# Attention and a token/channel mixer in one kernel: subtraction on VectorE, tiles in three pools, early reciprocals by way of DRAM

## The chip, the cores and the metric

The kernel runs on one core of one Trainium2 chip. The metric is the device time of one execution in microseconds, lower is better. A core has TensorE (PE, matmuls; its weight loads are listed as PEld), VectorE (DVE), ScalarE (ACT), GpSimd (POOL) and SyncE (SP), which here issues nearly all DMA transfers. Each runs its own list of instructions in order and waits on semaphores for the others. TensorE writes into PSUM, eight banks; all else lives in SBUF, 128 rows.

## The reference, cut to what matters

```
def phi(x):                                   # x: 8 batches, 8 heads, 576 tokens, 64
    proj = einsum('bhsd,df->bhsf', x, w_phi)  # 128 features
    proj = proj - max(abs(proj), axis=-1, keepdims=True)
    return concatenate([exp(proj), exp(-proj)], axis=-1)
q_p, k_p = phi(q), phi(k)
kv  = einsum('bhsf,bhsd->bhfd', k_p, v)
z   = sum(k_p, axis=2)
num = einsum('bhsf,bhfd->bhsd', q_p, kv)
den = einsum('bhsf,bhf->bhs', q_p, z)[..., None] + 1e-06
x   = num / den                               # heads side by side: 576 x 512
h   = relu(x.T @ w_tok1) @ w_tok2             # 576 -> 256 -> 576
u   = x + h.T
out = u + relu(u @ w_ch1) @ w_ch2             # 512 -> 1536 -> 512
```

All is float32, and the mixer's weights arrive as 64-bit floats.

## The kernel before, in words

Heads go in pairs: 32 pairs of two heads, four pairs to a batch. Five generators emit the program, and `weave` runs them side by side by shares written out by hand (each `yield` names a cost): `keys`, `queries`, `token_stream`, `load_weights`, `channel_stream`. The Tile framework then orders the instructions of each engine by its own simulated clock, so the final order on an engine is a planner's; an edit in one stage can shift the order in others.

*Attention.* For a group of two 128-token units, `less_max` multiplies by `w_phi` into PSUM, takes the largest absolute value of each row on VectorE (L226) and subtracts it. For the first four pairs (`i < PLAIN`) the product is one plain float32 matmul and stays in PSUM; `base` says which half of the rows holds the data, D for keys and 0 for queries. For the other pairs (`base is None`) both operands are split into a high and a low part of float32r, three fast matmuls replace one slow one (`mm3`), and the subtraction is a GpSimd instruction (L237) on a copy in SBUF.

For the plain pairs the subtraction goes another way. GpSimd negates the maximum (L229, two columns). For keys, ScalarE takes exp(proj - max) and exp(-proj + max) straight from PSUM with the negated or plain maximum as bias, one instruction for each unit and sign (L285). For queries, ScalarE writes proj - max with an Identity and a bias, one instruction for each unit (L235); TensorE transposes that and ScalarE takes the exponentials from PSUM (L371).

`add_kv` sums k_p and v over tokens into PSUM (L308) and copies the result to SBUF. `turn` and `numerators` give, for each half of a pair's tokens (k = 0: 320 tokens, k = 1: 256), the numerators and the denominators. For the first eight pairs (`i < EARLY`) ScalarE writes den with 1e-6 added (L406), later VectorE does (L408). Every denominator stands in 64 rows, one for each column of its head. When both heads are there (j == 1), VectorE takes the reciprocal of the whole 128 x 320 or 128 x 256 tile (L410) and GpSimd multiplies x by it (L411). den has one buffer.

*Weights.* `convert` loads a block of 64-bit floats into one of a few staging buffers (SP, L125), ScalarE takes the absolute value (L131), four VectorE instructions build the float32 (L132 to L135), ScalarE and GpSimd split it into high and low (`split`, L72 and L75). 33 such blocks are turned in the first part of the run, while the first pairs go through attention.

*Mixer.* `token_mix` needs all four pairs of a batch, `channel_mix` takes chunks of 256 tokens. Both are made of `mm3` (L81). They hold most of TensorE's work.

*Tiles.* Tiles that TensorE reads as its moving operand are made by `streamed`: 16 floats of padding on both sides. `column` rounds the small maxima up to 32 floats. Except for the constant pool all tiles lie in one pool, `wk`.

Of the kernel before, what the change touches and what calls it, by code (L numbers as in the profile page):

```python
# [8 lines left out]
F32 = mybir.dt.float32  # L9
F32R = mybir.dt.float32r  # L10
U32 = mybir.dt.uint32
# [6 lines left out]
P = 128  # L18
B, H, S, D = 8, 8, 576, 64
NP = H // 2  # L20
F = 128
# [21 lines left out]
def mixer_kernel(ctx, tc, qk, vm, vt, w_phi, w1, w2, wc1, wc2d, out):  # L43
    nc = tc.nc

    cst = ctx.enter_context(tc.tile_pool(name="cst", bufs=1))
    wk = ctx.enter_context(tc.tile_pool(name="wk", bufs=2))
    ps_w = ctx.enter_context(tc.tile_pool(name="ps_w", bufs=1, space=PSUM))
    ps_k = ctx.enter_context(tc.tile_pool(name="ps_k", bufs=1, space=PSUM))
# [3 lines left out]
    REST = dict(tag="rest", bufs=3)  # L53

    def streamed(pool, shape, dtype, **kw):

        n = 1
        for k in shape[1:]:
            n *= k
        t = pool.tile([P, n + 32], dtype, **kw)[:, 16:16 + n]  # L60
        if len(shape) == 3:
            t = t.rearrange("p (a b) -> p a b", a=shape[1])
        return t

    def column(pool, n, **kw):

        return pool.tile([P, 32], F32, **kw)[:, :n]

# [17 lines left out]
    make_identity(nc, ident)  # L86
    eps = cst.tile([P, 40], F32, name="eps")[:, :1]
    nc.gpsimd.memset(eps, 1e-6)
    wp2 = streamed(cst, [P, 2, F], F32R, name="wp2")
    wp = cst.tile([P, F], F32, name="wp")  # L90
# [5 lines left out]
    w1_l = cst.tile([P, 5, T], F32R, name="w1_l")  # L96
    w2_h = streamed(cst, [P, NT, S], F32R, name="w2_h")
    w2_l = streamed(cst, [P, NT, S], F32R, name="w2_l")
    wc1_h = cst.tile([P, NC_, E], F32R, name="wc1_h")
# [4 lines left out]
    for j in range(2):  # L104
        t = cst.tile([P, 672], F32, name=f"v{j}")[:, :650].rearrange("p (u j d) -> p u j d", u=5, j=2)
        nc.gpsimd.memset(t[:, 4], 0.0)
        nc.gpsimd.memset(t[:, 0:4, :, D:], 1.0)
        for i in range(2):
            nc.gpsimd.memset(t[i * D:(i + 1) * D, 4, i, D:], 1.0)
        vtiles.append(t)  # L110
# [3 lines left out]
    def convert(hi, lo, srcs, name, tag=None):  # L114
# [13 lines left out]
        top, low = raw[:, :, 1], raw[:, :, 0]  # L128
        m = streamed(wk, [P, 512], U32, tag="bits", name=f"bits{name}", bufs=3)[:w, :n]

# [60 lines left out]
    def less_max(ts, units, name, base=None):  # L191
# [25 lines left out]
        if base is None:  # L217
            part = wk.tile([P, 2, F], F32, tag="part", name=f"part{name}")
            nc.scalar.copy(part[:, :n], ps[:, :n, 1])
            pr = wk.tile([P, 2, F], F32, tag="p", name=f"p{name}")  # L220
            nc.vector.tensor_tensor(pr[:, :n], ps[:, :n, 0], part[:, :n], op=ALU.add)
            pr = pr[:, :n]
        else:
            pr = ps[:, :n, 0]
        mx = column(wk, 2, tag=f"mx{kind}", name=f"mx{name}")
        nc.vector.tensor_reduce(mx[:, :n], pr, axis=AX.X, op=ALU.max, apply_absolute_value=True)  # L226
        if base is not None:
            nmx = column(wk, 2, tag="nmx", name=f"nmx{name}")
            nc.gpsimd.tensor_scalar(nmx[:, :n], mx[:, :n], -1.0, None, op0=ALU.mult)  # L229
        if base == D:  # L230
            return pr, nmx, mx
        pm = wk.tile([P, 2, F], F32, tag=f"pm{kind}", name=f"pm{name}", bufs=1 if kind == "t" else 2)
        if base == 0:
            for i in range(n):
                nc.scalar.activation(pm[:, i], pr[:, i], AF.Identity, bias=nmx[:, i:i + 1])  # L235
        else:
            nc.gpsimd.tensor_tensor(pm[:, :n], pr, mx[:, :n].unsqueeze(2).to_broadcast([P, n, F]), op=ALU.subtract)  # L237
        return pm
# [23 lines left out]
    def keys():  # L262
        groups = [[(0, 0), (0, 1)], [(0, 2), (0, 3)], [(1, 0), (1, 1)], [(1, 2), (1, 3)], [None]]
        todo = None
        for i in range(B * NP):
# [11 lines left out]
            for g, us in enumerate(groups):  # L277
                pm = less_max(ts, us, f"k{i}_{g}", plain)
                kp = wk.tile([P, 2, 2, F], F32, tag="kp", name=f"kp{i}_{g}")
                for sg in range(2):  # L280
                    if i >= PLAIN:
                        nc.scalar.activation(kp[:, :len(us), sg], pm[:, :len(us)], AF.Exp, scale=1.0 - 2.0 * sg)  # L282
                        continue
                    for n in range(len(us)):
                        nc.scalar.activation(kp[:, n, sg], pm[0][:, n], AF.Exp, bias=pm[1 + sg][:, n:n + 1],  # L285
                                             scale=1.0 - 2.0 * sg)
                yield 0.22
                if todo:
                    add_kv(*todo)
                    yield 0.82  # L290
                todo = (i, g, us, kp, v_sb)
# [65 lines left out]
    def turn(i, k, j, pm, tail):  # L357
# [11 lines left out]
        for sg in range(2):  # L369
            full = wk.tile([P, SEG[0][1]], F32, tag="qf", name=f"qf{i}_{k}{j}{sg}")[:, :w]  # L370
            nc.scalar.activation(full, src, AF.Exp, scale=1.0 - 2.0 * sg)  # L371
            if i < PLAIN:
                qps.append(full)
                continue
            hi = streamed(wk, [P, SEG[0][1]], F32R, tag="qh", name=f"qh{i}_{k}{j}{sg}")[:, :w]
            lo = streamed(wk, [P, SEG[0][1]], F32R, tag="ql", name=f"ql{i}_{k}{j}{sg}")[:, :w]
            nc.scalar.activation(hi, src, AF.Exp, scale=1.0 - 2.0 * sg)  # L377
            (nc.gpsimd if sg else nc.vector).tensor_tensor(lo, full, hi.bitcast(F32), op=ALU.subtract)  # L378
            qps.append((hi, lo))
# [4 lines left out]
    def numerators(i, k, j, qps):  # L384
# [6 lines left out]
        if j == 0:  # L391
            dens[0] = wk.tile([P, SEG[0][1]], F32, tag="den", name=f"den{i}_{k}", bufs=1)[:, :w]
        den = dens[0]
# [15 lines left out]
        if j == 1:  # L409
            nc.vector.reciprocal(den, den)  # L410
            nc.gpsimd.tensor_tensor(x, x, den, op=ALU.mult)  # L411
            if k == 1:
                attended.add(i)
# [11 lines left out]
    def token_mix(b, h, xt):  # L425
        pa = bank(b, [P, NT, 256], f"pa{b}_{h}", 0)
        for u, (s0, w, _) in enumerate(UNITS):
# [5 lines left out]
            if w < P:  # L433

                xs = streamed(wk, [P, 2, P], F32R, tag="xh", name=f"xs{b}_{h}")
                nc.scalar.copy(xs[:w], px[:w])
# [8 lines left out]
                continue  # L445
            xh = streamed(wk, [P, 2, P], F32R, tag="xh", name=f"xh{b}_{h}_{u}")[:w]
            xl = streamed(wk, [P, 2, P], F32R, tag="xl", name=f"xl{b}_{h}_{u}")[:w]
            split(xh, xl, px[:w], nc.scalar, nc.vector)
# [22 lines left out]
    def channel_mix(i, segs):  # L471
        uh, ul = [], []
        for c in range(NC_):
            h = streamed(wk, [P, CH], F32R, tag=f"uh{c}", name=f"uh{i}_{c}", bufs=1)
            l = streamed(wk, [P, CH], F32R, tag=f"ul{c}", name=f"ul{i}_{c}", bufs=1)
            d = 0
# [10 lines left out]
        def up_proj(ep):  # L487
# [4 lines left out]
            for k in range(2):  # L492
                es = slice((2 * ep + k) * P, (2 * ep + k + 1) * P)
                for c in range(NC_):
                    mm3(ph[:, k], (wc1_h[:, c, es], wc1_l[:, c, es]), (uh[c], ul[c]), c == 0, c == NC_ - 1)
            gh = streamed(wk, [P, 2, CH], F32R, tag="g", name=f"gh{i}_{ep}", bufs=4)
            gl = streamed(wk, [P, 2, CH], F32R, tag="g", name=f"gl{i}_{ep}", bufs=4)
            nc.scalar.activation(gh, ph, AF.Relu)  # L498
# [120 lines left out]
```

## Time and profile before

| what | us |
|---|---|
| median of 3 runs | 1182.55 (1182.36 to 1184.48) |
| the profiled execution | 1180.86 |
| its span, first to last instruction | 1178.9 |
| TensorE busy in the span | 1134.0 |
| VectorE busy | 702.9 |
| ScalarE busy | 673.5 |
| GpSimd busy | 584.8 |

The profile is of one execution. Busy time is a union over an engine's instructions; idle time before an instruction is put down to what it waited for. Lines such as L410 are lines of the kernel before. "Granted clock" is the share of TensorE's full clock that its throttle allowed in that stretch. Matmuls are pipelined: 172 of them start in 20 us although each is recorded as 0.28 us long, so their rate is read from counts and not from durations.

### The profile page before, as it was taken

What the parts mean: (1) busy time and instruction counts of PE and PEld (TensorE: products, weight loads), DVE (VectorE), ACT (ScalarE), POOL (GpSimd) and SP (SyncE); (2) the same over time, 40 slices, a digit from 0 to 9 for tenths busy, and PEclk for the clock granted to TensorE, in tenths of its full rate; (3) what the DMA queues carried; (4) which work ended last, traced back from release to release, by engine and by line L of the source; (5) the groups of instructions that cost most, each with busy time, mean ns of one, the idle gap of its engine ahead of it and who ended that gap; (6) DMA issues with size and microseconds to landing.
All of it is one profiled execution on the core that took longest, in us unless ns stands there. A gap on an engine that the chain in (4) does not pass through costs nothing.

```text
span 1178.9 us, 24080 instructions
## 1 busy us (share of the span) xinstructions
PE 1134.0 (96%) x9032; PEld 1099.9 (93%) x9032; DVE 702.9 (60%) x1406; ACT 673.5 (57%) x1913; POOL 584.8 (50%) x774
## 2 busy tenths in 40 slices
PE   8877999999999999999999999999999999999998
PEld 6655889998999999998999999999999989999998
DVE  6899783566746666657656565474665666553111
ACT  6988784575746565566646455563665666441110
POOL 3567783465636564565546355462554655430000
PEclk9877799999999999999999999999999999999999
DMA  9543120111101111111111011110111110000000
GB/s 232 177 142 113 31 78 2 49 32 49 31 19 38 42 31 40 41 40 41 31 48 33 19 32 49 31 50 7 43 32 49 40 40 11 19 1 19 19 19 18
DMA packets 65299, 54.30 MB, mean 46 GB/s; under 512 B 44768, under 2 KB 56416, under 8 KB 65184
## 3 DMA queue, kind: packets, MB, share of 16 engines
q1 hardware_dynamic: 63824, 52.41, 15.4%
q8 instruction: 71, 1.16, 0.4%
q10 hardware_dynamic: 1360, 0.36, 0.1%
q14 instruction: 44, 0.36, 0.1%
HBM read 43.32 MB, written 9.44 MB: 45 GB/s over the span
## 4 chain that ended last, share of the span: by engine, by line
PE 84%; DVE 6%; ACT 6%; issue 2%; POOL 1%; DMA 1%; SPq 0%; POOLq 0%; DVEq 0%; ACTq 0%
PE acc L81 26%; PE h L81 26%; PE pkv L308 8%; PE pn L81 7%; PE ph L81 4%; PE pa L81 3%; PE pt L364 2%; PE ppk L212 2%; PE ppq L212 2%; DVE bitsc L135 1%; DVE bitsc L134 1%; PE px L432 1%; DVE bitsc L132 1%; ACT kp L285 1%; DVE den L410 1%
## 5 line engine op out<-in xcount | busy, mean ns | idle before, releaser
L81 PE MATMUL acc<-gh,wc 128*128 128x256 f32 x1728 | 339.7, 283 | 0.1
L81 PEld LDWEIGHTS acc<-gh,wc 128*128 128x128 f32 x1728 | 274.4, 188 | 0.4 <-ACT gh L498 0.4
L81 PE MATMUL h<-ul,wc_h 128*128 128x256 f32 x864 | 245.4, 284 | 1.9 <-POOL ul L479 1.8
L81 PE MATMUL h<-uh,wc_h 128*128 128x256 f32 x864 | 245.7, 285 | 0.5 <-DVE gl L499 0.5
L81 PE MATMUL h<-uh,wc_l 128*128 128x256 f32 x864 | 244.2, 283 | 0.0
L81 PE MATMUL acc<-gl,wc 128*128 128x256 f32 x864 | 243.2, 284 | 0.0
L308 PE MATMUL pkv<-v,kp 128*128 128x65 f32 (+1 forms) x1152 | 166.7, 280 | 6.9 <-ACT kp L285 4.3
L378 POOL TENSOR_TENSOR ql<-qf,qh 128x320 fp32r<-128x320 f32 (+1 forms) x112 | 93.0, 830 | 160.2 <-ACT qh L377 160.0
L308 PEld LDWEIGHTS pkv<-v,kp 128*128 128x128 f32 x1152 | 157.1, 202 | 14.6 <-ACT kp L285 7.9
L81 PEld LDWEIGHTS h<-ul,wc_h 128*128 128x128 f32 x864 | 162.8, 188 | 3.1 <-POOL ul L479 3.1
L81 PEld LDWEIGHTS h<-uh,wc_h 128*128 128x128 f32 x864 | 162.4, 188 | 1.1 <-DVE gl L499 1.1
L81 PEld LDWEIGHTS h<-uh,wc_l 128*128 128x128 f32 x864 | 163.2, 189 | 0.0
L81 PEld LDWEIGHTS acc<-gl,wc 128*128 128x128 f32 x864 | 162.9, 188 | 0.0
L499 DVE SCALAR_TENSOR_TENSOR gl<-h,gh 128x512 fp32r<-128x512 f32 x108 | 74.0, 685 | 144.1 <-ACT gh L498 143.1
L371 ACT ACTIVATE qf<-pt 128x320 f32<-128x320 f32 (+1 forms) x256 | 105.5, 416 | 85.9 <-PE pt L364 84.6
L282 ACT ACTIVATE kp<-pmk 128x256 f32<-128x256 f32 x280 | 96.0, 392 | 72.7 <-POOL pmk L237 69.6
L498 ACT ACTIVATE gh<-h 128x512 fp32r<-128x512 f32 x108 | 64.5, 598 | 112.8 <-PE h L81 112.1
L410 DVE RECIPROCAL den<-den 128x320 f32<-128x320 f32 x64 | 124.7, 1949 | 3.7 <-ACT den L406 2.3
L81 PE MATMUL pn<-qh,kv 128*128 128x320 f32 (+1 forms) x448 | 114.8, 297 | 0.6 <-ACT qh L377 0.3
L378 DVE TENSOR_TENSOR ql<-qf,qh 128x320 fp32r<-128x320 f32 (+1 forms) x112 | 70.1, 626 | 58.1 <-ACT qh L377 57.7
L237 POOL TENSOR_TENSOR pmk<-pk,mxk 128x256 f32<-128x256 f32 (+1 forms) x140 | 86.0, 614 | 35.7 <-DVE mxk L226 35.4
L187 POOL TENSOR_TENSOR stq<-raw,stq 64x512 fp32r<-64x512 f32 (+1 forms) x56 | 80.2, 1433 | 43.5 <-ACT stq L186 36.7
(112 smaller groups left out, 2418.4 us busy)
## 6 DMA issues: line engine op xcount, KB each, us to landing
raw<-in_qk SPq DMA_DIRECT2D x27, 576.0 KB, 3.8
rawc<-in_wc SPq DMA_DIRECT2D x24, 512.0 KB, 3.8
v<-in_vm SPq DMA_DIRECT2D x31, 256.0 KB, 3.4
out_x<-xt SPq DMA_DIRECT2D x12, 256.0 KB, 2.2
out_x<-xt SPq DMA_DIRECT2D x16, 192.0 KB, 2.0
raw<-in_w SPq DMA_DIRECT2D x8, 256.0 KB, 4.1
out_x<-xt SPq DMA_DIRECT2D x16, 128.0 KB, 1.9
pair<-in_qk SPq DMA_DIRECT2D x8, 160.0 KB, 4.5
```

Source lines behind the costliest of these rows:

```text
L81: nc.tensor.matmul(o, a, m, start=first and i == 0, stop=last and i == 2, skip_group_check=group_ok)
L187: nc.gpsimd.tensor_tensor(t[lo:lo + D], src, t[base:base + D].bitcast(F32), op=ALU.subtract)
L212: nc.tensor.matmul(ps[:, i].rearrange("p two f -> p (two f)"), t[:, c:c + P], wp2.rearrange("p two f -> p (two f)"), start=True, stop=True)
L237: nc.gpsimd.tensor_tensor(pm[:, :n], pr, mx[:, :n].unsqueeze(2).to_broadcast([P, n, F]), op=ALU.subtract)
L282: nc.scalar.activation(kp[:, :len(us), sg], pm[:, :len(us)], AF.Exp, scale=1.0 - 2.0 * sg)
L308: nc.tensor.matmul(o, kp[:, n, sg], v, start=g == 0 and n == 0 and sg == 0, stop=u is None, skip_group_check=True)
L364: nc.tensor.transpose(ptr[:, n], r, ident)
L371: nc.scalar.activation(full, src, AF.Exp, scale=1.0 - 2.0 * sg)
L378: (nc.gpsimd if sg else nc.vector).tensor_tensor(lo, full, hi.bitcast(F32), op=ALU.subtract)
L410: nc.vector.reciprocal(den, den)
L498: nc.scalar.activation(gh, ph, AF.Relu)
L499: nc.vector.scalar_tensor_tensor(gl, ph, 0.0, gh.bitcast(F32), op0=ALU.max, op1=ALU.subtract)
```

## The change

Three things change.

1. In `less_max` a plain pair's maximum is subtracted by one VectorE instruction for the whole group, from PSUM into SBUF; GpSimd's negation goes. Keys take the same two exponentials for a group as the later pairs do, from SBUF. Queries lose their Identity instructions.
2. For the first eight pairs the reciprocal is taken once for each denominator. Rows 0 and 64 of den are stored to DRAM, loaded back as a 128 x 5 or 128 x 4 tile (`few`), inverted by VectorE, stored again and loaded into all 64 rows of each half. All six transfers are issued by SP. den now has two buffers.
3. Padding goes. Moving operands lie in a pool `st`, tiles whose size is not a multiple of 512 bytes in a pool `odd`, the rest in `cst` and `wk`; two `lead` tiles, of 32 and 192 bytes, set where the pools begin. `bits` moves from the padded kind to `wk`; `qf`, the maxima, v, eps and den move to `odd`.

```
+    st = ctx.enter_context(tc.tile_pool(name="st", bufs=2))
+    odd = ctx.enter_context(tc.tile_pool(name="odd", bufs=2))
+    cst.tile([P, 8], F32, name="lead")
+    st.tile([P, 48], F32, tag="lead", name="lead2", bufs=1)
+    dr = ctx.enter_context(tc.tile_pool(name="dr", bufs=2, space=bass.MemoryType.DRAM))
...
-    wp2 = streamed(cst, [P, 2, F], F32R, name="wp2")
+    wp2 = st.tile([P, 2, F], F32R, tag="wp2", name="wp2", bufs=1)
...
-        t = cst.tile([P, 672], F32, name=f"v{j}")[:, :650].rearrange("p (u j d) -> p u j d", u=5, j=2)
+        t = odd.tile([P, 5, 2, D + 1], F32, tag=f"v{j}", name=f"v{j}", bufs=1)
...
-        m = streamed(wk, [P, 512], U32, tag="bits", name=f"bits{name}", bufs=3)[:w, :n]
+        m = wk.tile([P, 512], U32, tag="bits", name=f"bits{name}", bufs=3)[:w, :n]
...
-            pr = pr[:, :n]
+            pr, eng = pr[:, :n], nc.gpsimd
         else:
-            pr = ps[:, :n, 0]
-        mx = column(wk, 2, tag=f"mx{kind}", name=f"mx{name}")
+            pr, eng = ps[:, :n, 0], nc.vector
+        mx = odd.tile([P, 2], F32, tag=f"mx{kind}", name=f"mx{name}")
         nc.vector.tensor_reduce(mx[:, :n], pr, axis=AX.X, op=ALU.max, apply_absolute_value=True)
-        if base is not None:
-            nmx = column(wk, 2, tag="nmx", name=f"nmx{name}")
-            nc.gpsimd.tensor_scalar(nmx[:, :n], mx[:, :n], -1.0, None, op0=ALU.mult)
-        if base == D:
-            return pr, nmx, mx
         pm = wk.tile([P, 2, F], F32, tag=f"pm{kind}", name=f"pm{name}", bufs=1 if kind == "t" else 2)
-        if base == 0:
-            for i in range(n):
-                nc.scalar.activation(pm[:, i], pr[:, i], AF.Identity, bias=nmx[:, i:i + 1])
-        else:
-            nc.gpsimd.tensor_tensor(pm[:, :n], pr, mx[:, :n].unsqueeze(2).to_broadcast([P, n, F]), op=ALU.subtract)
+        eng.tensor_tensor(pm[:, :n], pr, mx[:, :n].unsqueeze(2).to_broadcast([P, n, F]), op=ALU.subtract)
         return pm
...
                 for sg in range(2):
-                    if i >= PLAIN:
-                        nc.scalar.activation(kp[:, :len(us), sg], pm[:, :len(us)], AF.Exp, scale=1.0 - 2.0 * sg)
-                        continue
-                    for n in range(len(us)):
-                        nc.scalar.activation(kp[:, n, sg], pm[0][:, n], AF.Exp, bias=pm[1 + sg][:, n:n + 1],
-                                             scale=1.0 - 2.0 * sg)
+                    nc.scalar.activation(kp[:, :len(us), sg], pm[:, :len(us)], AF.Exp, scale=1.0 - 2.0 * sg)
...
-            dens[0] = wk.tile([P, SEG[0][1]], F32, tag="den", name=f"den{i}_{k}", bufs=1)[:, :w]
+            dens[0] = odd.tile([P, SEG[0][1]], F32, tag="den", name=f"den{i}_{k}")[:, :w]
...
         if j == 1:
-            nc.vector.reciprocal(den, den)
+            if i < EARLY:
+                row, inv = (dr.tile([2, w], F32, tag=t, name=f"{t}{i}_{k}") for t in ("row", "inv"))
+                few = odd.tile([P, 8], F32, tag="few", name=f"few{i}_{k}")[:, :w // D]
+                for r in range(2):
+                    nc.sync.dma_start(row[r:r + 1], den[r * D:r * D + 1])
+                nc.sync.dma_start(few, row.rearrange("r (p c) -> (r p) c", c=w // D))
+                nc.vector.reciprocal(few, few)
+                nc.sync.dma_start(inv.rearrange("r (p c) -> (r p) c", c=w // D), few)
+                for r in range(2):
+                    nc.sync.dma_start(den[r * D:(r + 1) * D], inv[r:r + 1].to_broadcast([D, w]))
+            else:
+                nc.vector.reciprocal(den, den)
             nc.gpsimd.tensor_tensor(x, x, den, op=ALU.mult)
```

The other `streamed` tiles (w2, qh, ql, xh, xl, uh, ul, gh, gl) go to `st` in the same way.

More of the change, by code (lines that the diff above doesn't have):

```diff
@@ L53, in mixer_kernel @@
     REST = dict(tag="rest", bufs=3)
[L55 to L67, printed above, removed]
     def split(hi, lo, raw, eng_hi, eng_lo):
@@ L86, in mixer_kernel @@
     make_identity(nc, ident)
-    eps = cst.tile([P, 40], F32, name="eps")[:, :1]
+    eps = odd.tile([P, 1], F32, tag="eps", name="eps", bufs=1)
     nc.gpsimd.memset(eps, 1e-6)
-    wp2 = streamed(cst, [P, 2, F], F32R, name="wp2")
+    wp2 = st.tile([P, 2, F], F32R, tag="wp2", name="wp2", bufs=1)
     wp = cst.tile([P, F], F32, name="wp")
@@ L96, in mixer_kernel @@
     w1_l = cst.tile([P, 5, T], F32R, name="w1_l")
-    w2_h = streamed(cst, [P, NT, S], F32R, name="w2_h")
-    w2_l = streamed(cst, [P, NT, S], F32R, name="w2_l")
+    w2_h = st.tile([P, NT, S], F32R, tag="w2_h", name="w2_h", bufs=1)
+    w2_l = st.tile([P, NT, S], F32R, tag="w2_l", name="w2_l", bufs=1)
     wc1_h = cst.tile([P, NC_, E], F32R, name="wc1_h")
@@ L369, in turn @@
         for sg in range(2):
-            full = wk.tile([P, SEG[0][1]], F32, tag="qf", name=f"qf{i}_{k}{j}{sg}")[:, :w]
+            full = odd.tile([P, SEG[0][1]], F32, tag="qf", name=f"qf{i}_{k}{j}{sg}")[:, :w]
             nc.scalar.activation(full, src, AF.Exp, scale=1.0 - 2.0 * sg)
@@ L374, in turn @@
                 continue
-            hi = streamed(wk, [P, SEG[0][1]], F32R, tag="qh", name=f"qh{i}_{k}{j}{sg}")[:, :w]
-            lo = streamed(wk, [P, SEG[0][1]], F32R, tag="ql", name=f"ql{i}_{k}{j}{sg}")[:, :w]
+            hi = st.tile([P, 384], F32R, tag="qh", name=f"qh{i}_{k}{j}{sg}")[:, :w]
+            lo = st.tile([P, 384], F32R, tag="ql", name=f"ql{i}_{k}{j}{sg}")[:, :w]
             nc.scalar.activation(hi, src, AF.Exp, scale=1.0 - 2.0 * sg)
@@ L433, in token_mix @@
             if w < P:
-                xs = streamed(wk, [P, 2, P], F32R, tag="xh", name=f"xs{b}_{h}")
+                xs = st.tile([P, 2, P], F32R, tag="xh", name=f"xs{b}_{h}")
                 nc.scalar.copy(xs[:w], px[:w])
@@ L445, in token_mix @@
                 continue
-            xh = streamed(wk, [P, 2, P], F32R, tag="xh", name=f"xh{b}_{h}_{u}")[:w]
-            xl = streamed(wk, [P, 2, P], F32R, tag="xl", name=f"xl{b}_{h}_{u}")[:w]
+            xh = st.tile([P, 2, P], F32R, tag="xh", name=f"xh{b}_{h}_{u}")[:w]
+            xl = st.tile([P, 2, P], F32R, tag="xl", name=f"xl{b}_{h}_{u}")[:w]
             split(xh, xl, px[:w], nc.scalar, nc.vector)
@@ L473, in channel_mix @@
         for c in range(NC_):
-            h = streamed(wk, [P, CH], F32R, tag=f"uh{c}", name=f"uh{i}_{c}", bufs=1)
-            l = streamed(wk, [P, CH], F32R, tag=f"ul{c}", name=f"ul{i}_{c}", bufs=1)
+            h = st.tile([P, CH], F32R, tag=f"uh{c}", name=f"uh{i}_{c}", bufs=1)
+            l = st.tile([P, CH], F32R, tag=f"ul{c}", name=f"ul{i}_{c}", bufs=1)
             d = 0
@@ L495, in up_proj @@
                     mm3(ph[:, k], (wc1_h[:, c, es], wc1_l[:, c, es]), (uh[c], ul[c]), c == 0, c == NC_ - 1)
-            gh = streamed(wk, [P, 2, CH], F32R, tag="g", name=f"gh{i}_{ep}", bufs=4)
-            gl = streamed(wk, [P, 2, CH], F32R, tag="g", name=f"gl{i}_{ep}", bufs=4)
+            gh = st.tile([P, 2, CH], F32R, tag="g", name=f"gh{i}_{ep}", bufs=4)
+            gl = st.tile([P, 2, CH], F32R, tag="g", name=f"gl{i}_{ep}", bufs=4)
             nc.scalar.activation(gh, ph, AF.Relu)
```

## The prediction, made before the changed kernel ran

> **What bounds the kernel now.** The page came first: TensorE (PE) is busy for 96% of the span, so an engine change can pay only where PE is not full. Then busy time by stretch. The columns are the stretch, its length, busy us and instruction count of PE, PEld (weight loads), DVE (VectorE), ACT (ScalarE) and POOL (GpSimd), the granted TensorE clock, DMA share and GB/s.
>
> ```profile
> PE 1134.0 (96%) x9032; PEld 1099.9 (93%) x9032; DVE 702.9 (60%) x1406; ACT 673.5 (57%) x1913; POOL 584.8 (50%) x774
> 25.00:125.00 100.00, 82.43 (x378) 63.42 (x378) 93.88 (x143) 83.59 (x229) 63.07 (x72) 0.76 0.47 141
> 125.00:175.00 50.00, 45.34 (x321) 41.84 (x321) 38.68 (x80) 41.99 (x118) 40.59 (x47) 0.93 0.20 54
> 175.00:225.00 50.00, 50.00 (x423) 49.82 (x422) 21.14 (x42) 23.62 (x67) 18.34 (x27) 1.00 0.06 23
> 45.00:127.00 82.00, 63.89 (x294) 49.12 (x294) 79.32 (x117) 67.79 (x181) 53.07 (x56) 0.77 0.41 125
> 125.00:1178.90 1053.90, 1031.48 (x8572) 1.00 0.11 33
> ```
>
> From 125 us on PE works for 1031 of 1054 us at full clock (the last row is a view of PE alone). Before that it is slow and waiting: in 45 to 127 us VectorE works for 79.3 of 82 us while PE has 64 us at clock 0.77. So there are two kernels: a start bound by VectorE, and a rest bound by PE. Whatever brings the end of the start forward by 1 us brings the end of the program forward by about 1 us; a VectorE us saved later is worth nothing by itself. The chain of work over the first 125 us says the same:
>
> ```profile
> by line: DVE bitsc L134 10.1%; issue 8.0%; DVE bitsc L132 7.8%; DVE bitsc L135 7.5%; ACT kp L285 7.1%; DVE den L410 6.4%; PE pkv L308 5.3%; DVE bitsc L133 5.2%; PE pn L398 5.2%; DMA rawc<-in_wc 4.5%; DMA pair<-in_qk 3.6%; PE ppq L216 3.1%;
> ```
>
> Four VectorE steps of the weight conversion (L132 to L135) lead it; the reciprocal (L410) holds 6.4% of 125, 8.0 us, and the plain pairs' exponentials (L285) 8.9 us. Grouped by line in 25 to 125 us (busy us, mean ns; then idle time before it):
>
> ```profile
> L134 DVE SCALAR_TENSOR_TENSOR bitsc<-rawc,bitsc 128x512 uint32<-128x512 uint32 x23 | 20.5, 890 | 0.2
> L135 DVE SCALAR_TENSOR_TENSOR bitsc<-rawc,bitsc 128x512 uint32<-128x512 uint32 x21 | 18.4, 877 | 0.2
> L132 DVE TENSOR_SCALAR bitsc<-bitsc 128x512 f32<-128x512 f32 x23 | 15.9, 692 | 1.6 <-ACT bitsc L131 1.6
> L410 DVE RECIPROCAL den<-den 128x320 f32<-128x320 f32 (+1 forms) x8 | 15.5, 1942 | 0.0
> L131 ACT ACTIVATE bitsc<-rawc 128x512 f32<-128x512 f32 x23 | 15.5, 677 | 3.6 <-DMA rawc<-in_wc 2.0 <-POOL wc L75 1.6
> L133 DVE TENSOR_SCALAR bitsc<-bitsc 128x512 uint32<-128x512 uint32 x23 | 14.9, 649 | 0.2
> L226 DVE TENSOR_REDUCE mxk<-ppk 128x2 f32<-128x256 f32 (+1 forms) x14 | 5.4, 385 | 1.7 <-PE ppq L216 0.9 <-PE ppk L216 0.8
> L226 DVE TENSOR_REDUCE mxq<-ppq 128x2 f32<-128x256 f32 x12 | 5.0, 415 | 2.1 <-PE ppq L216 2.1
> ```
>
> **The change part by part.**
>
> *Reciprocals of pairs 0 to 7.* Sixteen wide reciprocals go; eight of them, 15.5 us, lie in the VectorE-bound stretch. Each is replaced by one over 128x5 or 128x4, which the trace does not show. The two wide forms differ by 399 ns for 64 columns, 6.2 ns a column, which leaves 153 ns at zero columns: an estimate of 184 and 178 ns, 1.5 us for eight. Between 0 and the 1.5 it matters little. VectorE gains 14.0 us there. The other eight lie after 125 us, where PE is full: worth 0, covered by PE's own queue.
>
> ```profile
> L410 DVE RECIPROCAL den<-den 128x320 f32<-128x320 f32 x32 | 68.7, 2148 | 1.9 <-ACT den L406 1.4
> L410 DVE RECIPROCAL den<-den 128x256 f32<-128x256 f32 x32 | 56.0, 1749 | 1.8 <-ACT den L406 0.9
> L221 DVE TENSOR_TENSOR pk<-ppk,partk 128x256 f32<-128x256 f32 x112 | 46.2, 412 | 10.0 <-POOL pmt L237 4.5 <-ACT partk L219 3.3 <-POOL pmk L237 0.9
> L226 DVE TENSOR_REDUCE mxt<-ppt 128x1 f32<-128x128 f32 x4 | 1.1, 272 | 0.0
> ```
>
> *Subtraction on VectorE.* Pairs 0 to 3 get one subtraction for each maximum. A VectorE operation from PSUM and SBUF takes 412 ns at 128x256 (L221), as long as the maximum (415), so I price each subtraction as its own reduction: 5.4 + 5.0 + three of mxt at 0.27 = 11.2 us in 25 to 125 us; eleven more fall before 25 us, where VectorE has room. VectorE's net there: 11.2 - 14.0 = -2.8 us. Giving with one hand what the other takes is the centre of this change.
>
> *What leaves ScalarE and GpSimd.*
>
> ```profile
> 25.00:125.00 100.00, 13.33 (x32) 0.76 0.47 141
> L132 DVE TENSOR_SCALAR bits<-bits 128x512 f32<-128x512 f32 x2 | 0.8, 423 | 1.5 <-ACT bits L131 1.5
> L133 DVE TENSOR_SCALAR bits<-bits 128x512 uint32<-128x512 uint32 x2 | 0.8, 419 | 0.0
> L134 DVE SCALAR_TENSOR_TENSOR bits<-raw,bits 128x512 uint32<-128x512 uint32 x2 | 1.4, 680 | 0.0
> L135 DVE SCALAR_TENSOR_TENSOR bits<-raw,bits 128x512 uint32<-128x512 uint32 x2 | 1.4, 681 | 0.0
> by line: DMA rawc<-in_wc 12.4%; PE pkv L308 10.2%; DMA pair<-in_qk 10.0%; PE pn L398 10.0%; ACT kp L285 9.2%; PE ppk L216 5.4%; issue 4.7%; PE ppq L216 4.1%; POOL w_l L75 3.9%; SPq L256 3.1%; POOL nmxk L229 2.5%; DVE bitsc L133 2.3%; ACT bi
> ```
>
> The first row is L229 alone, GpSimd's negation: 13.3 of its 63.1 us. Two prices hang on it. The conversion steps take 692, 649, 890 and 877 ns in this stretch and 423, 419, 680 and 681 ns in the same shape early on: 23 x 269 + 23 x 230 + 23 x 210 + 21 x 196 ns = 20.4 us lost. If that is GpSimd in the way, its negations' share is at most 20.4 x 13.3 / 63.1 = 4.3 us; at least 0. The negations carry two columns, so most of their time is their own wait; I take 1.5 us. The second price is the first 45 us (last row, the chain there): kp 9.2% and nmxk 2.5% are 4.1 + 1.1 us. Two exponentials of 128x256 in place of four of 128x128 save about a third of the first (1.4), the negation goes, the subtraction adds about as much as three or four groups of 0.41: I take -1.0, ends -2.5 and 0. After 45 us ScalarE has room (67.8 of 82), so what it loses there counts 0; its cover is VectorE itself.
>
> The Trainium skill has a rule on the first price (SBUF — State Buffer, "Who interferes with whom"): a VectorE instruction with two SBUF inputs, or in a two-port mode, fully blocks against a GpSimd instruction that reads SBUF, whole instruction against whole instruction. By it every negation removed frees VectorE and the sum would be up to 2.8 us lower; the new subtraction, with one input in PSUM, would not contend. No row here separates the two.
>
> *The way by DRAM.* Per half pair SP issues six transfers: two row stores, a spread load, a spread store, two broadcast loads: 96 in all. Their nearest rows are the 16 KB loads, quoted for 25 to 125 us and for 60 to 80 us, and 64 KB output stores.
>
> ```profile
> v<-in_vt SPq DMA_DIRECT2D x7, 16.0 KB, 2.3
> v<-in_vt SPq DMA_DIRECT2D x2, 16.0 KB, 3.8
> out_x<-xt SPq DMA_DIRECT2D x16, 64.0 KB, 1.8
> 45.56 1.23 SPq L274 DMA_DIRECT2D v<-in_vt  x2
> SPq L125 <- DVE bitsc L135: 54.4, 16, 8.6
> rawc<-in_wc SPq DMA_DIRECT2D x21, 512.0 KB, 3.8
> 127.59 1.06 POOL L411 TENSOR_TENSOR xt<-xt,den 128x256 f32<-128x256 f32 x1
> 137.07 0.38 PE L432 MATMUL px<-ident,xt 128*128 128x128 f32 x2
> ```
>
> Issue takes 0.6 us each, 3.7 us of SP per half pair, eight in 100 us. SP has that time: in the first 300 us it waits 54 us for staging buffers alone. The chain of four landings is 4 x 1.8 to 4 x 3.8 plus issue, 11 to 19 us in place of 2 us. Three costs follow. (a) SP is in order: behind each of its three waits stand the 512 KB weight loads. Four staging buffers and a load of 3.8 us against one conversion each 4.3 us (23 in 100) leave about 9 us of cover: 0. (b) VectorE is in order: behind the small reciprocal, if its load is late, stand the conversions. Late by nothing: 0; two landings each 3.8 instead of 2.3: 3.0 us x 8 = 24 us. I take 2.0 us over the eight, because in this stretch the only engine wait on 21 loads of weights is 2.0 us (L131 above): the order of instructions mostly puts consumers behind landings. (c) GpSimd's multiplication now waits for the DMA, and behind it stand the splits that free staging. Pair 3's last half is scaled from 127.6 to 128.7 us and its transposes start at 137.1: 8.4 us of room against a chain at least 9 us longer. Other pairs' matmuls lie ready there: 0, upper end +4.
>
> *Tiles apart.* By the tile sizes, the tiles that PE streams stood 64 bytes past a multiple of 128 relative to the others (16 floats of padding ahead), and they still do (leads of 32 and 192 bytes); the second buffer of den frees ScalarE earlier. At most 9032 matmuls x 1 ns = 9 us either way, but groups that read different tiles differ by 1 to 2 ns, and the last stretches go at 116 ns a matmul whatever buffer is read: 0.
>
> ```profile
> L81 PE MATMUL acc<-gh,wc 128*128 128x256 f32 x1728 | 339.7, 283 | 0.1
> L81 PE MATMUL h<-ul,wc_h 128*128 128x256 f32 x864 | 245.4, 284 | 1.9 <-POOL ul L479 1.8
> 1105.00:1125.00 20.00, 20.00 (x172) 1.00 0.09 27
> ```
>
> **Sum.** -2.8 (VectorE net) - 1.5 (conversions less disturbed) - 1.0 (first 45 us) + 2.0 (waits for the spread load) = -3.3 us. The profiled execution took 1180.86 us (span 1178.9), so 1177.6; it lies 1.69 us under the median of the runs, 1182.55, which gives 1179.3 us as the median after.
>
> **Rivals.**
> 1. *The waits eat the gain and more (slower).* Place: VectorE in 45 to 127 us, at the small reciprocal. The gain without waits is 5.3 us over eight half pairs, so it turns at 0.7 us a half pair. If half of the 24 us comes, 12 - 5.3 = +6.7: 1189 us. For it: landings of 3.8 us in the busy stretch, VectorE with no idle time to give. Against it: 2.0 us of waits on loads now.
>  The Trainium skill speaks for this one (DMA: Bandwidth & Descriptors, "Latency and other measured facts"): HBM access is 0.2 us on average and 2 us under high load, and each hop pays the round trip. By it the four hops under load would be some 7 us longer, an estimate; the 16 KB rows above, 2.3 against 3.8 us, show a smaller step.
> 2. *Much faster.* The reciprocal leaves the chain whole (8.0 us), half of the exponentials' 8.9 us too, and the subtractions slip into the pauses that shorter ScalarE work opens: 8.0 + 4.4 - 2 = -10.4: 1172 us. For it: ScalarE at 84 of 100 us falls. Against it: VectorE has no pauses, and 11.2 us of new work there is sure.
> 3. *It does nothing measurable.* VectorE's 2.8 us are won, but PE, granted 0.77 of its clock there, and the late scaling of pair 3 hold the start's end; or the other order of instructions costs what is won: 1182.5 us, within 2.4.
>
> **How the numbers follow.** A measurement here tells about 0.2%, 2.4 us. Forecast (1 to 6.5 us faster) 0.40; slower 0.25; much faster 0.15; nothing 0.20. Of the forecast's case 0.07 lies within 0.2%: faster 0.48, same 0.27, slower 0.25. The likeliest case's own range is 1176 to 1181.5. The range for 8 in 10 takes in rival 2's 1172 and most of rival 1: 1171 to 1190 us.
>
> **What would show it.** VectorE in 25 to 125 us: eight operations of about 0.18 us in place of 15.5 us, 29 subtractions of 0.27 to 0.42. L132 to L135 means below 692, 649, 890, 877. Waits of VectorE on the spread load: some 2 us; over 6 us means rival 1. PE full from some 122 us on instead of 125. The prediction is wrong if VectorE idles in 45 to 127 us, if the matmul pace leaves 116 ns, or if the gain or loss lies after 175 us.

## The result and the profile after

The changed kernel took 1165.61 us (median of 4 runs, 1164.33 to 1171.54) against 1182.46 us for the kernel before: ratio 0.9872 (95%: 0.9853 to 0.9890), 1.3% faster. The prediction said 1179.3 us, with 1171 to 1190 as its range; the median lies 5.4 us below that range. The profiled execution took 1164.33 us.

The page's list of busy time, after. TensorE runs as many matmuls as before, x9032, and is busy 12.7 us less:

```profile
PE 1121.3 (96%) x9032; PEld 1090.5 (94%) x9032; DVE 685.7 (59%) x1446; ACT 659.4 (57%) x1845; POOL 570.1 (49%) x734
```

Busy time by stretch, after (columns as in the prediction). VectorE is as busy as before in 25 to 125 us (in 45 to 127 us it works 75.7 of 82 us, before 79.3); ScalarE and GpSimd lost 9.5 and 11.0 us there:

```profile
25.00:125.00 100.00, 86.54 (x415) 69.82 (x415) 93.50 (x182) 74.05 (x180) 52.07 (x42) 0.92 0.56 161
```

The granted clock in this row, 0.92, is too high. This trace has no record of the clock before 58.3 us, the column counts time without a record as 1.00, and TensorE goes at half pace there (last section). With half clock until 58.3 us the stretch comes to 0.76. Before, where the records begin at 27.3 us, the same reckoning gives 0.75.

Groups by line of the same stretch, after. The conversion steps are now L125 to L128, the subtraction L221, the multiplication of x L402:

```profile
L128 DVE SCALAR_TENSOR_TENSOR bitsc<-rawc,bitsc 128x512 uint32<-128x512 uint32 x23 | 20.2, 879 | 0.0
L126 DVE TENSOR_SCALAR bitsc<-bitsc 128x512 uint32<-128x512 uint32 x23 | 19.1, 830 | 0.1
L127 DVE SCALAR_TENSOR_TENSOR bitsc<-rawc,bitsc 128x512 uint32<-128x512 uint32 x23 | 18.1, 789 | 0.1
L125 DVE TENSOR_SCALAR bitsc<-bitsc 128x512 f32<-128x512 f32 x23 | 14.5, 634 | 2.9 <-ACT bitsc L124 2.9
L402 POOL TENSOR_TENSOR xt<-xt,den 128x320 f32<-128x320 f32 (+1 forms) x7 | 6.4, 915 | 11.2 <-DMA den<-inv 11.0
L221 DVE TENSOR_TENSOR pmq<-ppq,mxq 128x256 f32<-128x256 f32 x13 | 5.3, 409 | 0.1
L221 DVE TENSOR_TENSOR pmk<-ppk,mxk 128x256 f32<-128x256 f32 (+1 forms) x13 | 4.9, 379 | 0.0
```

The small reciprocal over the whole span (min, median, max in ns), and VectorE's waits in 25 to 125 us, after; none is for the spread load:

```profile
L396 DVE RECIPROCAL few<-few x16: 161/172/191, 46.7 to 258.8; 128x5 f32<-128x5 f32 x8, 128x4 f32<-128x4 f32 x8
```

```profile
DVE bitsc L125 <- ACT bitsc L124: 2.9, 5, 1.2
DVE mxk L219 <- PE ppk L209: 2.4, 3, 1.0
DVE mxq L219 <- PE ppq L209: 0.5, 1, 0.5
DVE pmt L221 <- PE pt L343: 0.2, 1, 0.2
```

The chain of work over the first 125 us, after. The conversions are no longer at its head, and the way by DRAM stands in it with 12.6%:

```profile
by line: PE pkv L287 16.8%; PE pn L377 10.8%; PE ppk L209 10.5%; DMA inv<-few 9.8%; PE ppq L209 6.4%; issue 5.5%; DVE bitsc L127 4.8%; PE pt L343 3.1%; DVE bitsc L128 3.0%; DMA few<-row 2.8%; DVE bitsc L126 2.8%; DMA wp<-in_w_phi 2.5%; DVE 
```

TensorE alone from 175 to 1075 us, before and then after. The number in brackets counts the matmuls in the same 900 us, at full clock and with TensorE busy in both:

```profile
175.00:1075.00 900.00, 886.20 (x7407) 1.00 0.12 34
```

```profile
175.00:1075.00 900.00, 884.73 (x7471) 1.00 0.12 34
```

64 more matmuls in 900 us, some 7.5 us at 118 ns each, is a gain after the start, where the prediction put none. It is about half of what this execution gained; the other half came in the start. TensorE from 75 to 175 us, before and after:

```profile
75.00:175.00 100.00, 84.95 (x494) 0.83 0.28 83
```

```profile
75.00:175.00 100.00, 86.04 (x569) 0.91 0.37 101
```

From 0 to 175 us 77 more matmuls run (858 against 781), an estimate of 9 us; the experiments show that this part comes in some executions only. To see the size of the later part, starts are read instead of durations. The *spacing* below is the mean distance from the start of one 128x256 matmul to the next start, worked out from the start times in the trace between 175 and 1050 us, distances over 130 ns left out. Before it is 117.73 ns, in one broad heap from 113 to 122. After it is 115.84 ns, in two narrow heaps: 47% lie under 115.5 ns, nearly all of these at 113 or 114, and most others at 117 to 119. 5144 of them by 1.89 ns are 9.7 us.

### The profile page after: what moved, and what is told of

Same layout as the page of the kernel before. It is cut to its first block, busy times and chain, and to the rows that moved or that the text cites. A ratio compares the mean times of both kernels' runs of the same rounds, so it can differ in the third digit from the quotient of the medians.

```text
span 1162.2 us, 24135 instructions
## 1 busy us (share of the span) xinstructions
PE 1121.3 (96%) x9032; PEld 1090.5 (94%) x9032; DVE 685.7 (59%) x1446; ACT 659.4 (57%) x1845; POOL 570.1 (49%) x734
## 4 chain that ended last, share of the span: by engine, by line
PE 85%; ACT 5%; DVE 4%; DMA 3%; issue 1%; POOL 1%; SPq 0%; POOLq 0%; DVEq 0%; ACTq 0%
PE acc L74 25%; PE h L74 25%; PE pkv L287 9%; PE pn L74 7%; PE ph L74 4%; PE pa L74 3%; PE pt L343 3%; PE ppk L205 2%; PE ppq L205 2%; DMA inv<-few 1%; PE px L423 1%; PE pn L377 1%; PE ppk L209 1%; ACT qh L356 1%; ACT qf L350 1%
## 5 line engine op out<-in xcount | busy, mean ns | idle before, releaser
L265 ACT ACTIVATE kp<-pmk 128x256 f32<-128x256 f32 (+1 forms) x320 | 109.3, 392 | 89.0 <-POOL pmk L221 83.7
L402 POOL TENSOR_TENSOR xt<-xt,den 128x320 f32<-128x320 f32 x64 | 53.8, 840 | 116.7 <-DVE den L401 36.6
L221 POOL TENSOR_TENSOR pmk<-pk,mxk 128x256 f32<-128x256 f32 (+1 forms) x140 | 86.8, 620 | 30.0 <-DVE mxk L219 23.2
```

The lines of the kernel that those rows point to most:

```text
L221: eng.tensor_tensor(pm[:, :n], pr, mx[:, :n].unsqueeze(2).to_broadcast([P, n, F]), op=ALU.subtract)
```

## The experiments

**Which part?** One run changes the tiles alone, one has everything but the tiles. Edit of the first: the pools `st`, `odd` and the two leads as in the change, nothing else. Of the second: the change with `streamed`, `column` and the two pools of before.

> The kernel before with the tiles in three pools as after, and nothing else: the order of instructions on every engine is that of the kernel before. Theory P, placement sets the pace of TensorE: in the trace after, 256-column matmuls that follow each other start 115.5 to 116.3 ns apart on average in 300 to 1030 us, in the trace before 117.7 ns, and the lead of after grows from 8 to 17 us there. So this kernel takes 1172 to 1176 us, its matmuls stand 115.5 to 116.5 ns apart after 300 us, and its first 130 us are those of before. Rival Q, the pace comes with the instructions and their order: 1182 us, 117.7 ns.

> Subtraction on VectorE and the reciprocals by way of DRAM, tiles placed as before; the order of instructions on every engine is that of the kernel after. Theory P: the gain of the first 130 us stays (8 to 11 us), the pace is 117.7 ns: 1172 to 1175 us. Rival Q: all of the gain stays, 1165 to 1167 us, at 115.5 to 116.5 ns.

Tiles alone: 1170.89 us, 0.9909 (0.9886 to 0.9932). All but the tiles: 1174.64 us, 0.9971 (0.9947 to 0.9995). TensorE from 175 to 1075 us, tiles alone and then all but the tiles:

```profile
175.00:1075.00 900.00, 885.86 (x7483) 1.00 0.12 34
```

```profile
175.00:1075.00 900.00, 885.04 (x7388) 1.00 0.12 34
```

Spacing 115.98 and 117.76 ns. The order of instructions of the first is that of the kernel before on every engine, that of the second that of the changed one. So the faster pace comes with the tiles and not with the order: some 0.9% of the 1.3%, -10.7 us (0.0091 of 1180.7) against -3.4 us for all the rest. Theory P had both spacings right; the tiles alone came out 1.1 us under its range. The two parts add up to -14.1 us; the whole change, by its ratio, is -15.1.

**The two parts of the rest.** The subtraction alone, and the way by DRAM alone, tiles as before.

```
subtraction alone:  eng.tensor_tensor(pm, pr, mx, op=subtract)   # eng = nc.vector for plain pairs; L410 stays
DRAM alone:         if i < EARLY: row, few, inv by DRAM          # negation and biases stay
```

> The subtraction on VectorE alone. Theory S, VectorE's work bounds the first 125 us: 29 subtractions add 10 to 11 us there and nothing is taken off it: 1188 to 1194 us. Rival L, latency bounds it (maximum, GpSimd's negation, four ScalarE instructions): one VectorE and two ScalarE instructions in their place shorten the way of each group, 1172 to 1180 us.

> The reciprocals by way of DRAM alone. Theory S: 14 us less VectorE work in 25 to 125 us, less some waits: 1168 to 1174 us. Rival L: the path of a group is unchanged and the scaling comes later: 1181 to 1186 us.

Subtraction alone: 1182.51 us, 1.0014 (1.0002 to 1.0027). DRAM alone: 1187.58 us, 1.0049 (1.0033 to 1.0065). Busy time from 25 to 125 us, subtraction alone and then DRAM alone:

```profile
25.00:125.00 100.00, 77.97 (x416) 61.66 (x414) 97.77 (x167) 71.86 (x178) 50.14 (x42) 0.86 0.47 144
```

```profile
25.00:125.00 100.00, 81.96 (x355) 62.82 (x354) 78.82 (x142) 83.05 (x225) 61.33 (x71) 0.69 0.51 149
```

Neither run fell in a range that its theories gave: the subtraction alone lies between S and L, DRAM alone 1.6 us above L. With the subtraction alone attention goes ahead (416 matmuls instead of 378) but VectorE is at 97.8 of 100, and the weights come late: the last VectorE step of the thirtieth of 31 conversions (the trace shows 31; the 33 of the section on the kernel before is wrong) starts at 140.5 us, before at 126.0. With DRAM alone VectorE has 21 us free, and the wait has moved to GpSimd: it stands 13.4 us for the broadcast loads before it can multiply x (L424), and behind that multiplication stand the splits that free staging buffers. ScalarE's first conversion step waits 5.3 us for these splits, VectorE's first step 7.5 us for ScalarE. In the chain of work over the first 125 us the four kinds of landing hold 23.0%, in the changed kernel the two that its line shows hold 12.6%. Fewer matmuls start (355). The two parts together start 414. Each part alone gains nothing; they gain only together. One rival is open: in these two runs the planner's order is neither that of before nor that of after, and what the order alone costs was not measured.

**Moving or stationary operand?** A matmul has a stationary operand (its weights) and a moving one. By the addresses in the built kernels, which the traces do not hold, before: stationary operands at 32 mod 128 and moving ones at 96 mod 128 bytes of a partition, both at several places mod 512. After: all stationary ones at 160 mod 512 and all moving ones at 352, a distance of 192, which is the size of lead2. Four runs disturb that while the instructions and their order stay.

```
mixed moving:     each tile of pool st 128 bytes longer       # 96, 224, 352, 480 mod 512
mixed wc2:        each wc2 tile of cst 128 bytes longer       # 160, 288, 416, 32
distance 128:     lead2 [P, 48] -> [P, 32]                    # moving at 288
distance 0:       lead2 [P, 48] -> [P, 128]                   # moving at 160
```

> The kernel after with 128 bytes more for each tile of the pool of moving operands, so that these start at four places modulo 512 bytes (96, 224, 352, 480) as they did before, and at one place (352) after; the order of instructions is that of after. Theory M, TensorE's spacing of 113 ns needs all moving operands at one place modulo 512: the spacing goes back to 117.7 ns on average in 300 to 1030 us, the time to 1172 to 1176 us. Rival N, the place of the stationary operands counts: nothing changes, 1164 to 1168 us, 115.5 to 116.5 ns.

> The kernel after with 128 bytes more for each of eight wc2 tiles, stationary operands of the down projection, which then start at four places modulo 512 (160, 288, 416, 32) where after has one (160); the order of instructions is that of after. Theory M: nothing changes, 1164 to 1168 us, 115.5 to 116.5 ns. Rival N: the spacing is 117.7 ns in the groups that write acc at least, 1168 to 1174 us.

> The kernel after with the second lead tile 64 bytes shorter: all moving operands start at 288 modulo 512 in place of 352, the stationary ones stay at 160; the order is that of after. Theory M (one place for all is what counts): as after, 1164 to 1168 us, 113 and 118 ns mixed. Rival O, the distance to the stationary operands counts, 64 modulo 128 being the good one: spacing of 117.7 ns or more, 1172 us or more.

> The kernel after with the second lead tile 320 bytes longer: moving and stationary operands all start at 160 modulo 512; the order is that of after. Theory M: as after, 1164 to 1168 us. Rival O: 117.7 ns or more, 1172 us or more; both operands at the same place should be the worst case of a conflict between their reads.

TensorE from 175 to 1075 us, in this order:

```profile
175.00:1075.00 900.00, 884.71 (x7386) 1.00 0.13 35
```

```profile
175.00:1075.00 900.00, 883.45 (x7474) 1.00 0.12 34
```

```profile
175.00:1075.00 900.00, 886.48 (x7356) 1.00 0.13 35
```

```profile
175.00:1075.00 900.00, 886.02 (x7316) 1.00 0.12 35
```

Mixing the moving operands over four places takes the whole gain of pace away (1177.1 us, 1.1 above theory M's range; 0.9973, 0.9950 to 0.9995; spacing 117.75 ns); mixing one stationary group does not (0.9855, 0.9796 to 0.9915; 115.60 ns). That second run says more than its mean: of the matmuls that read the eight mixed tiles, those whose own weights lie at a distance of 64 or 320 start 115.3 ns apart, those at 192 or 448 start 115.2 ns apart (672 and 662 between 175 and 1050 us, told apart by the order in which `channel_mix` reads the tiles). A lead of 64 bytes less makes the kernel slower than before (1.0054, 1.0027 to 1.0080; 118.89 ns), a distance of 0 more so (1.0077, 1.0045 to 1.0108; 119.66 ns). So one common place is not enough: theory M fell in these two runs, and rival O held. The next runs ask whether M holds at a distance of 64 mod 128.

**Which distance?** Only lead2 changes, so only the place of the moving operands.

```
distance 64: [P, 16]    distance 320: [P, 80]    distance 448: [P, 112]    distance 256: [P, 64]
```

> The changed kernel with the first tile of the pool of moving operands 128 B per partition shorter: all moving operands stand at 224 mod 512 instead of 352, the stationary ones at 160 as before, so the distance is 64 mod 512 and still 64 mod 128. The order of instructions on every engine is that of the changed kernel. Theory M (it is enough that all moving operands share one place mod 512, with a distance of 64 mod 128 from the stationary ones): as the changed kernel, matmuls of 256 columns at 113 to 118 ns apart with a mean of 115 to 116 between 500 and 800 us, 1163 to 1170 us. Theory N (it is the distance of 192 mod 512 that is good): 117.7 ns or more throughout, 1174 us or more.

> The changed kernel with the first tile of the pool of moving operands 128 B per partition longer: moving at 480 mod 512, stationary at 160, distance 320 mod 512 (64 mod 128 and 64 mod 256). Theory M (one place mod 512, distance 64 mod 128): as the changed kernel, mean spacing 115 to 116 ns between 500 and 800 us, 1163 to 1170 us. Theory N (distance of 192 mod 512, or mod 256): 117.7 ns or more, 1174 us or more.

> The changed kernel with the first tile of the pool of moving operands 256 B per partition longer: moving at 96 mod 512, stationary at 160, distance 448 mod 512 (64 mod 128 and 192 mod 256). Theory M (one place mod 512, distance 64 mod 128): as the changed kernel, 115 to 116 ns, 1163 to 1170 us. Theory N with the distance of 192 taken mod 256: as the changed kernel too; taken mod 512: 117.7 ns or more, 1174 us or more.

> The changed kernel with the first tile of the pool of moving operands 64 B per partition longer: moving at 416 mod 512, stationary at 160, distance 256 mod 512, which is 0 mod 128. Theory M (the distance mod 128 decides, and 0 is bad): as the runs with distance 0 and 128 were, 118.9 to 119.7 ns and 1184 to 1192 us. A rival in which only a distance of 0 or 128 mod 512 is bad: 113 to 118 ns, 1163 to 1175 us.

Theory M fell at 64 and 320, theory N held in its form mod 256: distances 64 and 320 behave alike, 448 like 192, 256 like 0. It is the distance mod 256 that sorts them. N was not exact: 64 and 320 keep about a tenth of the 113 ns matmuls and came out at 117.3 ns, not at 117.7; distance 64 took 1172.2 us, 1.8 us under N's range.

**Distance, or the moving operand's own place?** The first lead and lead2 change together, so the tiles of the pools ahead of `st` move, all stationary operands of the mixer among them, and the moving operands stay; the third run lets the moving ones alternate between 352 and 96, both 192 mod 256 away.

```
stationary at 224: lead [P, 8] -> [P, 24], lead2 [P, 48] -> [P, 32]     # distance 128
stationary at 288: lead [P, 8] -> [P, 40], lead2 [P, 48] -> [P, 16]     # distance 64
two good places:   each tile of pool st 256 bytes longer                # 352 and 96
```

> The changed kernel with the stationary and plain tiles 64 B per partition further on (at 224 mod 512 instead of 160) and the moving operands where they were (352): the distance is now 128, 0 mod 128. The order of instructions is that of the changed kernel. Theory D (the distance between moving and stationary operand counts, and 0 mod 128 is bad): no 113 ns matmuls, a mean of 118.8 ns or more between 500 and 800 us, 1180 to 1192 us. Theory A (the moving operand's own place counts): as the changed kernel, 115 to 116 ns, 1160 to 1172 us.

> The changed kernel with the stationary and plain tiles 128 B per partition further on (at 288 mod 512) and the moving operands where they were (352): distance 64. Theory D in the form that a distance of 192 mod 256 is better than one of 64 mod 256: few 113 ns matmuls as in the runs with the moving operands at 224 and 480, a mean of 117.1 to 117.5 ns between 500 and 800 us, 1170 to 1182 us. Theory A (the moving operand's own place, 96 mod 256, counts): as the changed kernel, 115 to 116 ns, 1160 to 1172 us.

> The changed kernel with each tile of the moving pool 256 B per partition longer, so that the moving operands alternate between 352 and 96 mod 512, the two places that by themselves had 40 to 50 % of 113 ns matmuls. If only the poorer places (224 and 480) spoil a mix: as the changed kernel, 115 to 116 ns between 500 and 800 us, 1160 to 1172 us. If different places in a row spoil it: as with four places, 117.7 ns, 1172 to 1184 us.

With the moving operands left where they were, the move of the other pools alone brings the poor pace. TensorE from 175 to 1075 us, the three in order:

```profile
175.00:1075.00 900.00, 885.26 (x7334) 1.00 0.12 35
```

```profile
175.00:1075.00 900.00, 884.37 (x7405) 1.00 0.12 34
```

```profile
175.00:1075.00 900.00, 883.57 (x7444) 1.00 0.13 35
```

So the distance between the pool of moving operands and the other pools counts, and not the moving operands' own place; mixing two places is harmless when both are at 192 mod 256. That a matmul's distance to its own weights is what counts is not shown, and mixed wc2 speaks against it. Then the steps between, to see whether it is graded:

```
distance 160: lead2 [P, 48] -> [P, 40]        distance 224: lead2 [P, 48] -> [P, 56]
```

> The changed kernel with the first tile of the pool of moving operands 32 B per partition shorter: moving operands at 320 mod 512, stationary at 160, distance 160. If the effect goes by steps of 64 B (a distance of 160 counts as 128): 118.9 ns between 175 and 1050 us, 1180 to 1190 us. If it is graded: between 128 and 192, some 117.4 ns, 1172 to 1182 us. If a distance off the multiples of 64 is free of it: 113.3 ns or 115 ns at most, 1150 to 1165 us.

> The changed kernel with the first tile of the pool of moving operands 32 B per partition longer: moving operands at 384 mod 512, stationary at 160, distance 224. If the effect goes by steps of 64 B (a distance of 224 counts as 192): 116 ns between 175 and 1050 us, 1160 to 1172 us. If it is graded: between 192 and 256, some 117.8 ns, 1172 to 1184 us. If a distance off the multiples of 64 is free of it: 115 ns at most, 1150 to 1165 us.

All runs with one distance, and those with several:

| moving minus stationary, bytes | mod 256 | spacing, ns | share under 115.5 ns | ratio to before (95%) |
|---|---|---|---|---|
| 0 | 0 | 119.66 | 0.5% | 1.0077 (1.0045 to 1.0108) |
| 256 | 0 | 119.66 | 0.6% | 1.0106 (1.0050 to 1.0163) |
| 64 | 64 | 117.27 | 13% | 0.9937 (0.9908 to 0.9966) |
| 320 | 64 | 117.37 | 11% | 0.9962 (0.9931 to 0.9992) |
| 64, stationary moved | 64 | 117.22 | 14% | 0.9949 (0.9926 to 0.9972) |
| 128 | 128 | 118.89 | 14% | 1.0054 (1.0027 to 1.0080) |
| 128, stationary moved | 128 | 118.91 | 14% | 1.0032 (1.0008 to 1.0055) |
| 160 | 160 | 118.38 | 9% | 0.9975 (0.9947 to 1.0002) |
| 192 (the changed kernel) | 192 | 115.84 | 47% | 0.9872 (0.9853 to 0.9890) |
| 448 | 192 | 116.09 | 42% | 0.9892 (0.9837 to 0.9948) |
| 192 and 448 mixed | 192 | 116.15 | 41% | 0.9932 (0.9910 to 0.9955) |
| 224 | 224 | 118.35 | 8% | 0.9992 (0.9965 to 1.0020) |
| 64 and 192 mixed, as before | both | 117.76 | 14% | 0.9971 (0.9947 to 0.9995) |
| 64 and 192 mixed, one stationary place | both | 117.75 | 11% | 0.9973 (0.9950 to 0.9995) |

All rows have the subtraction and the way by DRAM. 160 and 224 came out at 118.4 ns where the graded case had expected 117.4 and 117.8: no good place lies between, and none of the other eight distances beats the change's own. Mixed wc2 had the lowest single time, 1157.86 us, but its interval holds the changed kernel's ratio, so no better version is shown.

**The changed kernel again**, beside the kernel before on one chip.

> The changed kernel once more, beside the kernel before on one chip. If its start has two courses, as in the runs of subtraction with the reciprocals by way of DRAM: two groups of times 8 to 10 us apart, told apart by the granted clock (0.983 or more, and 0.979 or less), around 1165 and 1172 us. If not: 1164 to 1168 us throughout. The spacing of the matmuls after 300 us as before, 115 to 116 ns between 500 and 800 us.

1166.77 us, 0.9895 (0.9862 to 0.9929). The spacing was 116.16 ns. Two things are to be seen. First, the pace at one distance is one of two, and either can hold for long: from 1080 to 1100 us, where the same matmuls run without a pause, the first execution and then the second:

```profile
1080.00:1100.00 20.00, 20.00 (x172) 1.00 0.10 28
```

```profile
1080.00:1100.00 20.00, 20.00 (x178) 1.00 0.10 28
```

Worked out from the starts between 1075 and 1150 us, the spacing is 117.78 and 113.33 ns: the same kernel in the same stretch, once at the longer pace to the end and once at the shorter one. In the first execution, between 175 and 1050 us, of 159 changes from the shorter to the longer 113 came at the first matmul after one of another shape or after a pause, and 157 within one matmul of that; 133 of 159 changes back came inside a series.

Second, the start has two courses. The mean granted clock tells them apart, though it counts the time before the first record as full clock. The four runs lay at 1162.6 and 1163.8 (mean granted clock 0.987 and 0.984) and at 1169.7 and 1170.9 (0.976 and 0.974). All but the tiles shows it best: seven runs around 1173.3 at 0.984 or more, five around 1182.8 at 0.977 or less. The kernel before had nothing over 0.981. TensorE in two stretches of the start, first the changed kernel's execution of 1164 us, then one at distance 320 with the other course:

```profile
28.00:36.00 8.00, 8.00 (x31) 1.00 0.73 227
60.00:76.00 16.00, 12.58 (x82) 0.98 0.63 196
```

```profile
28.00:36.00 8.00, 7.53 (x54) 1.00 0.68 216
36.00:40.00 4.00, 0.49 (x4) 0.78 0.66 205
60.00:76.00 16.00, 16.00 (x58) 0.50 0.45 147
```

The second is quick at 28 us, runs out of work from 36 to 40 and is at half clock from 60 to 76; the first is slow at 28 and quick from 60. The records of the clock show how much this is. Of the 16 profiled executions with both the subtraction and the way by DRAM, ten have the full clock from 57 to 60 us on, for 17 us; six have half clock until 79 to 82 us. Counting the time before the first record as half, half clock before 176 us is 60 to 77 us in the ten and 89 to 97 us in the six. So it is not only where the half clock falls that differs, but how much there is. What chooses the course was not tested.

## Why the prediction was wrong

- **Tiles apart, 0 us: the step that failed.** Measured alone, -10.7 us (-13.5 to -8.0), against "9 us either way" as its bound. The prediction saw the bound and chose 0 because "groups that read different tiles differ by 1 to 2 ns". But all groups of the kernel before read mixed places, so they could not show what one common place does. It also noted that the change keeps the distance mod 128 and took this for no change; the runs show that mod 256 counts, where before mixed 64 with 192 and after has 192 alone. All its signs of being wrong came true in part: the mean spacing fell from 117.73 to 115.84 ns, about half of the profiled execution's gain lay after 175 us, and VectorE worked 75.7 of 82 us in 45 to 127 us instead of 79.3.
- **The rest, -3.3 us: near in sum by luck, not by its working.** All but the tiles measured -3.4 us (-6.3 to -0.6). By the prediction's terms the subtraction alone (11.2 - 1.5 - 1.0) should have cost 8.7 us and DRAM alone (-14.0 + 2.0) gained 12.0; both cost, 1.7 and 5.8 us. VectorE's work was sized well: 0.17 us a reciprocal against 0.18, 11.1 us for the 29 subtractions of L221 against 11.2, 78.8 us busy with DRAM alone against 93.9 - 14 = 79.9. What failed is that a VectorE us saved in the start is a us off the end: with DRAM alone the freed time was worth nothing while the chain by DRAM, GpSimd and ScalarE held. And -3.4 is a mean over the two courses, about -7 and +2.
- **Conversions less disturbed, -1.5 us: no relief seen.** The four steps took 634, 830, 789 and 879 ns, 3132 in sum against 3108 before, although GpSimd was busy 11.0 us less. With the subtraction alone, the cleaner test, they took 3248. The rule of the Trainium skill that was weighed there (SBUF — State Buffer, "Who interferes with whom") would have had the removed negations free VectorE; no such relief shows here. What made the steps longer was not tested.
- **Waits at the spread load, +2.0 us: 0** up to 125 us, and 3.5 us with DRAM alone. The wait came at GpSimd instead (11.0 us at L402), which step (c) had foreseen and priced at 0; pair 3's last scaling ended at 133.66 us and its transposes started at 133.71, so the 8.4 us of room were used up.
- **First 45 us, -1.0 us:** no run separates it.
- **Rivals.** The time came out below rival 2's 1172 us, but by another way: in the quicker course all but the tiles gained about 7 of rival 2's 10.4 us, and the tiles, which no rival had, gave the rest. The wide reciprocal left the chain, as rival 2 had it, and DMA landings (12.6% of 125 us, 15.8 us) took its place. Rival 1's waits at VectorE did not come.

## What to carry to other kernels

In a kernel that keeps TensorE full, give the moving operands a pool of their own, so that one tile ahead of it sets where all of them lie relative to the other pools, and measure some distances: here it moved the time from 0.987 to 1.011 with the same instructions. Read the pace from counts of starts in equal stretches, since recorded durations (282 ns against 283) hide it. When two changes share a stretch, run each alone before adding their prices: here neither paid without the other. Before comparing granted clocks, see where a trace's records of it begin.

## What the runs showed of the hardware

- The pace of float32r matmuls of 256 columns, each with its own weights, depends on where the pool of moving operands lies relative to the other pools, mod 256 bytes: 115.8 to 119.7 ns at full granted clock. The Trainium skill (SBUF — State Buffer, "Who interferes with whom") lists TensorE's two read ports as independent. Under that rule alone no distance between the two operands would matter; the placement does matter here, but that it acts through these two ports is not shown. Two runs speak against a rule that goes matmul by matmul: in mixed wc2 the matmuls at 64 mod 256 kept 115.3 ns, and moving operands mixed over 64 and 192 take 117.75 ns where the mean of 117.3 and 115.8 would be 116.6. Left open too: why one distance has two paces, 113 and 118 ns.
- The column of the granted clock says 1.00 where the trace has no record of the clock. The first record lies at 58.3 us in the changed kernel's trace and at 28.0 us in the one at distance 320. From 28.6 us on the same line starts a matmul each 213 ns in the first (2.66 us for 12 as recorded) and each 112 ns in the second (1.90 for 16), and the column says 1.00 for both:

```profile
28.64 2.66 PE L287 MATMUL pkv<-v,kp 128*128 128x65 f32 x12
```

```profile
28.34 1.90 PE L287 MATMUL pkv<-v,kp 128*128 128x65 f32 x16
```

- Where the half clock falls differs between executions of one kernel. The Trainium skill (TensorE: Matmul & The Clock Gate, "What's actually happening") says that the gate's window runs freely and that the number of cold matmuls varies from run to run; the two courses agree with it. It puts the ramp's price under 1% of a typical span. Here the steps from one matmul to the next at half pace, within 12%, add up to 50 us before 176 us; at full pace they would take half, so the price is some 25 us of 1162, 2.2%, an estimate that takes none of these steps to be held up by anything else.
